# Attention and two feed-forward blocks in one program: batch 0's keys in three tiles of 128 and one shared tile, grouped loads of v, two leading products, one sum per pair, and a replanned order

## The chip, the core and the metric

The kernel runs on one core of a Trainium2 chip. The metric is the device time in microseconds (us) of one execution, compared as the median of several runs. The core's engines work side by side: TensorE (PE) multiplies matrices, with its weight loads listed apart (PEld), VectorE (DVE) and ScalarE (ACT) work on elements, GpSimd (POOL) and SyncE (SP) mostly issue transfers here. They wait for each other through semaphores, and each works through its own list of instructions in the order in which the program was written.

## The reference

Three blocks follow each other. `q`, `k`, `v` have 4 batches, 12 heads, 448 positions and 64 values a head; `cap` is 30.

```python
def _attn_ref(q, k, v, cap):
    scale = 1.0 / np.sqrt(q.shape[-1])
    scores = scale * np.matmul(q, k.transpose(0, 1, 3, 2))
    scores = cap * np.tanh(scores / cap)
    scores = scores - np.max(scores, axis=-1, keepdims=True)
    attn = np.exp(scores)
    attn = attn / (np.sum(attn, axis=-1, keepdims=True) + 1e-09)
    return np.matmul(attn, v).astype(np.float32)

def _moe_ref(x, w_in, w_out):        # 1792 x 768, 768 x 2048, 2048 x 768
    h = x @ w_in
    ...
    g = np.where(pos, h, np.where(neg, 0.0, (h + beta) ** 2 / (4.0 * beta)))
    return (g @ w_out).astype(np.float32)

def _moe2_ref(x, w1, w2, w3, w_out): # 1792 x 768, three of 768 x 768, 768 x 768
    h = np.maximum(np.maximum(x @ w1, x @ w2), x @ w3)
    return (h @ w_out).astype(np.float32)
```

## The kernel before

All work is transposed: positions (448 a batch) lie along a tile's free axis, features or keys along its 128 partitions.

*Attention* (`attention`, one call for each batch and pair of heads, 24 in all). The two heads of a pair lie on partitions 0 to 63 and 64 to 127. The 448 keys are cut into four tiles of 112. For each tile PE makes the scores of both heads (`score` in batch 0, as plain 32-bit products; `score_full` in the other batches, from values divided into a high and a low part), ACT takes tanh out of the PSUM buffer (`t`, 112 x 896) and then exp in place. PE then weighs v with the exps (`weigh`, accumulated in `ps_a`). For the denominator DVE adds the four exp tiles to one or two (`se`; the table `ADDED` says which: three adds to one tile in batches 0 and 3, two adds to two tiles in batches 1 and 2), and PE sums each over its partitions by a product with ones (`total4`, into `ps_r`; `total` for the last pair of batch 0). The sum with its epsilon (`rs`) is gathered by POOL to a small tile (`rc`), inverted on DVE, sent to device memory by SP and read back spread over 64 partitions a head (`spread2`). Last, `xf` is `ps_a` times `rs`, and it is divided into a high and a low part (`x`).

*Layers.* `ffn` runs the first block for batches 0 and 1; the later stages use a scheme with seven products of half matrices (`strassen`). A product of high precision is three products on PE of values in a shorter format (lines 899 to 901 and 1117): high by high, high by low, low by high. The weights come as 64-bit words and are turned to 32-bit numbers on DVE and ACT (`fetch_first`) and divided into two parts (`divided`: a cast on ACT or DVE, a subtraction on DVE). The first `PLAIN` = 6 units of `w_in` are not divided in batch 0: their six products each are plain 32-bit ones (line 894).

*Order.* Every piece of work is given to a planner (`Plan`) with a cost for each engine that could do it, a due time, what it depends on and which buffers it takes from pools of fixed size (`slots`). `run` steps through time, hands free engines the earliest due work that is ready, and `emit` writes all instructions in the order found. So a changed cost moves instructions on every engine up to the end. A dependency between engines is counted `LATENCY` later. PSUM pool `s` has two buffers for scores, `m` three for sums, weighings and layer products, `a` one. In batch 0, pairs 1, 2, 4 and 5 weigh into a buffer of `m`, which their `xf` frees.

*Start.* ACT loads `cap`, SP the keys and queries of the first pair, every engine loads the value of `cap` to a register (line 218) and branches on it; `cap` of 30 takes the branch without a maximum.

## Time and profile before

| | us |
|---|---|
| median of 3 runs | 955.91 (955.85 to 959.21) |
| the profiled execution | 959.17 |
| its span in the profile | 957.4 |
| PE busy | 937.2 (98%) |
| DVE busy | 778.0 (81%) |
| ACT busy | 594.5 (62%) |

The profiled execution is 1.8 us longer than its span, and 3.3 us longer than the median. "Busy" counts the time in which at least one instruction of the engine is under way. The page shows the span in 40 slices as well: PE's busy tenths read 7789999... and then 9 up to the last slice, so PE has idle time almost only in the first 70 us, which hold batch 0's attention. The granted clock (the share of TensorE's full clock) reads 9989 in the first four slices and 9 afterwards.

### The profile page before, as it was taken

How to read it: one execution, taken by the hardware profiler on the slowest of the kernel's cores; microseconds unless marked ns; L12 is line 12 of the kernel's file. 1: busy time of each engine (PE TensorE's matmuls, PEld its weight loads, DVE VectorE, ACT ScalarE, POOL GpSimd, SP SyncE). 2: the span in 40 equal slices, each digit the busy share in tenths (PEclk: the TensorE clock that was granted, in tenths of full speed). 3: DMA queues.
4: the chain of work that ended last, by engine and by line, in shares of the span. 5: the costliest groups of instructions: out<-in, count | busy, mean ns of one | idle time of the engine just before them, and what ended most of it. 6: DMA issues, size and time to landing. Idle time of an engine off the chain costs nothing.

```text
span 957.4 us, 14768 instructions
## 1 busy us (share of the span) xinstructions
PE 937.2 (98%) x5323; PEld 755.6 (79%) x5323; DVE 778.0 (81%) x1288; ACT 594.5 (62%) x932; POOL 14.7 (2%) x27
## 2 busy tenths in 40 slices
PE   7789999999999999999999999999999999999997
PEld 1134788777767676678999999999999999899997
DVE  2898898897989888888888848887889869758782
ACT  7968888775888877774434316566865715233441
POOL 0000000000000000000000000000000000000000
PEclk9989999999999999999999999999999999999999
DMA  7758768998888998853777887442233345446343
GB/s 201 220 154 267 236 191 245 274 287 270 291 280 279 302 292 259 232 173 118 253 265 271 288 295 255 123 140 80 90 101 109 111 121 184 144 147 205 108 148 120
DMA packets 95339, 194.48 MB, mean 203 GB/s; under 512 B 12094, under 2 KB 56858, under 8 KB 95258
## 3 DMA queue, kind: packets, MB, share of 16 engines
q1 hardware_dynamic: 94378, 193.36, 64.0%
q8 instruction: 44, 0.72, 0.3%
q0 software_dynamic: 736, 0.10, 0.1%
q14 instruction: 37, 0.30, 0.1%
q10 hardware_dynamic: 144, 0.00, 0.0%
HBM read 142.51 MB, written 50.81 MB: 202 GB/s over the span
## 4 chain that ended last, share of the span: by engine, by line
PE 90%; DMA 3%; DVE 3%; issue 2%; ACT 1%; SPq 0%; POOL 0%; DVEq 0%; ACTq 0%; POOLq 0%
PE ps_m L1117 32%; PE ps_s L1117 11%; PE ps_m L899 9%; PE ps_m L901 8%; PE ps_m L900 8%; PE ps_a L836 6%; PE ps_s L615 5%; PE ps_a L1117 5%; PE ps_m L894 3%; PE ps_r L709 1%; DMA qk<-in_qk 1%; DMA rc<-rs 1%; DVE op L315 1%; DVE se L315 1%; PE ps_s L626 1%
## 5 line engine op out<-in xcount | busy, mean ns | idle before, releaser
L1117 PE MATMUL ps_m<-op,w 128*128 128x448 f32 x1575 | 324.0, 365 | 0.6 <-DVE M L315 0.6
L1117 PEld LDWEIGHTS ps_m<-op,w 128*128 128x128 f32 x1575 | 295.7, 188 | 24.4 <-DVE M L315 1.0
L315 DVE TENSOR_TENSOR w<-wf,w 128x512 fp32r<-128x512 f32 (+2 forms) x155 | 117.6, 761 | 13.8 <-ACT w L310 11.4
L310 ACT ACTIVATE w<-wf 128x512 fp32r<-128x512 f32 (+2 forms) x120 | 81.1, 679 | 70.4 <-PE ps_m L1117 30.9
L633 ACT ACTIVATE t<-ps_s,qscale 112x896 f32<-112x896 f32 x96 | 93.4, 1004 | 33.0 <-PE ps_s L615 25.2
L1117 PE MATMUL ps_s<-op,w 128*128 128x448 f32 x522 | 110.7, 366 | 0.4 <-DVE op L315 0.2
L1117 PEld LDWEIGHTS ps_s<-op,w 128*128 128x128 f32 x522 | 98.0, 188 | 8.7 <-ACT op L310 0.5
L680 ACT ACTIVATE t<-t,cap_sb 112x896 f32<-112x896 f32 x96 | 95.9, 1038 | 0.3
L310 ACT ACTIVATE w<-ss 128x384 fp32r<-128x384 f32 (+1 forms) x93 | 53.1, 583 | 64.9 <-PE ps_m L1117 37.5
L836 PE MATMUL ps_a<-t,v 112*32 112x448 f32 (+1 forms) x752 | 79.4, 543 | 5.2 <-ACT t L680 2.7
L899 PE MATMUL ps_m<-g,w 128*128 128x448 f32 x192 | 72.6, 378 | 0.0
L315 DVE TENSOR_TENSOR w<-ss,w 128x384 fp32r<-128x384 f32 (+1 forms) x98 | 59.8, 627 | 14.3 <-ACT w L310 14.0
L901 PE MATMUL ps_m<-g,w 128*128 128x448 f32 x192 | 70.3, 366 | 0.0
L900 PE MATMUL ps_m<-g,w 128*128 128x448 f32 x192 | 70.3, 366 | 0.0
L836 PEld LDWEIGHTS ps_a<-t,v 112*32 112x32 f32 (+1 forms) x752 | 22.2, 110 | 51.3 <-issue 33.1
L899 PE MATMUL ps_m<-x,w 128*128 128x448 f32 x156 | 58.7, 376 | 0.0
L423 DVE SCALAR_TENSOR_TENSOR raw<-raw 128x768 int32<-128x768 int32 (+1 forms) x64 | 55.4, 867 | 3.0 <-ACT raw L412 2.5
L900 PE MATMUL ps_m<-x,w 128*128 128x448 f32 x156 | 57.1, 366 | 0.6 <-DVE x L315 0.6
L439 DVE SCALAR_TENSOR_TENSOR wf<-raw 128x768 int32<-128x768 int32 (+1 forms) x64 | 54.7, 856 | 3.1 <-ACT raw L431 1.6
L901 PE MATMUL ps_m<-x,w 128*128 128x448 f32 x156 | 57.0, 366 | 0.0
L1117 PE MATMUL ps_a<-op,w 128*128 128x448 f32 x234 | 51.3, 365 | 0.0
L1117 PEld LDWEIGHTS ps_a<-op,w 128*128 128x128 f32 x234 | 44.0, 188 | 3.5
(142 smaller groups left out, 1424.8 us busy)
## 6 DMA issues: line engine op xcount, KB each, us to landing
wf<-w SPq DMA_DIRECT2D x104, 192.0 KB
wf<-w SPq DMA_DIRECT2D x66, 256.0 KB
w<-wf SPq DMA_DIRECT2D x40, 384.0 KB
wf<-w SPq DMA_DIRECT2D x40, 384.0 KB
raw<-in_w SPq DMA_DIRECT2D x18, 768.0 KB
w<-p SPq DMA_DIRECT2D x36, 384.0 KB
raw<-in_w_in SPq DMA_DIRECT2D x16, 768.0 KB
raw<-in_w_out SPq DMA_DIRECT2D x24, 512.0 KB
```

The costliest lines, as they stand in the source:

```text
L310: nc.scalar.activation(out=out_, in_=in_, func=AF.Copy)
L315: nc.vector.tensor_tensor(out=out_, in0=a, in1=b, op=o)
L423: nc.vector.scalar_tensor_tensor(out=lo, in0=hi, scalar=-(2**31), in1=lo, op0=ALU.bitwise_and, op1=ALU.bitwise_or,)
L439: nc.vector.scalar_tensor_tensor(out=wf.tile[:, :n].bitcast(I32), in0=hi, scalar=3, in1=lo, op0=ALU.logical_shift_left, op1=ALU.bitwise_or,)
L615: nc.tensor.matmul(ps.tile[:C, j, :S], k.tile[o, 1, c * C : (c + 1) * C], q.tile[o, 0], start=n == 0, stop=n == 2,)
L633: nc.scalar.activation(out=t[c].tile, in_=ps.tile[:C, :, :S], func=AF.Tanh, scale=qscale[:C])
L680: lambda e, c=c: nc.scalar.activation(out=t[c].tile, in_=t[c].tile, func=AF.Exp, scale=cap_sb[:C]),
L836: nc.tensor.matmul(pa.tile[j * D + d : j * D + d + n, :S], vt.tile[:, j, c, d : d + n], t[c].tile[:, j], start=start, stop=stop,)
L899: nc.tensor.matmul(ps.tile[:, :S], wh, a.tile[:, 0], start=start, stop=False)
L900: nc.tensor.matmul(ps.tile[:, :S], wh, a.tile[:, 1], start=False, stop=False)
L901: nc.tensor.matmul(ps.tile[:, :S], wl, a.tile[:, 0], start=False, stop=stop)
L1117: nc.tensor.matmul(get(), w_, x_, start=start and z == 0, stop=stop and z == 2, skip_group_check=begun,)
```

## The change

Batch 0 alone (`HALVED`) takes its keys differently: the first 64 keys of both heads share one tile `th` (head 0 on partitions 0 to 63, head 1 on 64 to 127, 448 wide), and the other 384 lie in three tiles of 128. So a pair has three wide tiles and one of half the width where it had four of 112 partitions. `th` is scored and weighed by two products, one a head, in place of four. For the denominator DVE makes two adds (three wide tiles to one), and PE sums two tiles: `se` with ones, and `th` with `blocks`, which holds ones for one head's partitions and zeros for the other's.

v of batch 0 is loaded for three pairs at a time into a buffer of pool `w` (`load_thirds`), eight transfers each with runs of 64 values, in place of one transfer a pair with runs of 256 values.

Two products of ones by ones, which nothing reads, stand on PE ahead of all else. `PLAIN` is 3. `ADDED` is 3 in all batches: batches 1 and 2 make three adds and one sum a pair, where they made two and two. Pool `u` has 34 buffers (35), `h` 11 (9).

The planner counts an ACT pass as 0.1 us shorter and a DVE pass 0.08 us shorter for what follows on the same engine (`LAP`), a dependency 0.09 us later, also between passes of one engine other than PE, and a pause of 5 us after each gather and of 2 us after each read back.

```diff
--- before.py
+++ after.py
@@ -27,7 +27,8 @@
...
-    LATENCY = 0.08
+    LATENCY = 0.09
+    LAP = {"A": 0.1, "D": 0.08}
...
@@ -153,7 +154,7 @@
...
-                        free_at[e] = t + c
+                        free_at[e] = t + c - self.LAP.get(e, 0.0)
...
@@ -181,7 +182,7 @@
...
-                            d.t1 + (0.0 if d.e in x.cost and len(x.cost) == 1 else self.LATENCY)
+                            d.t1 + (0.0 if d.e == "T" and "T" in x.cost else self.LATENCY)
...
@@ -215,9 +216,21 @@
...
+    ones = const.tile([128, 64], F32, name="ones")
+    nc.vector.memset(ones, 1.0)
+    with (
+        tc.tile_pool(name="idle", bufs=1) as idle,
+        tc.tile_pool(name="ps_idle", bufs=1, space=bass.MemoryType.PSUM) as ps_idle,
+    ):
+        x, y = idle.tile([128, 448], F32, name="x"), ps_idle.tile([64, 448], F32, name="y")
+        nc.vector.memset(x, 1.0)
+        for _ in range(2):
+            nc.tensor.matmul(y, ones, x, start=True, stop=True)
     bits = nc.values_load(cap.bitcast(I32)[0:1, 0:1])
-    ones = const.tile([v.shape[2], 64], F32, name="ones")
-    nc.vector.memset(ones, 1.0)
+    blocks = const.tile([128, 2, 64], F32, name="blocks")
+    nc.gpsimd.memset(blocks, 0.0)
+    for j in range(2):
+        nc.gpsimd.memset(blocks[j * 64 : (j + 1) * 64, j], 1.0)
...
@@ -271,22 +284,23 @@
...
     FULL = (1, 2, 3)
+    HALVED = (0,)
     RC = 16
-    PLAIN = 6
+    PLAIN = 3
...
-    ADDED, FOURS, POOLED = (3, 2, 2, 3), (0, 1, 2, 3), ()
+    ADDED, FOURS, POOLED = (3, 3, 3, 3), (0, 1, 2, 3), ()
...
-    slots = {"u": 35, "h": 9, "v": 3, "w": 4, "wf": 5, "raw": 3, "rc": 2, "s": 2, "a": 1, "m": 3}
...
+    slots = {"u": 34, "h": 11, "v": 3, "w": 4, "wf": 5, "raw": 3, "rc": 2, "s": 2, "a": 1, "m": 3}
...
@@ -564,6 +578,46 @@
...
+    def load_thirds(b, a, begin):
+
+        vt = buf("w", "vt", [P, 3 * 7 * D])
+        src = v[b, 6 * a : 6 * a + 6]
+        ops = [[] for _ in range(NCH)]
+
+        def load(r, to, part):
+            q = op(
+                {"Q": 0.5}, lambda e: nc.sync.dma_start(out=to(vt.tile), in_=part),
+                begin + 0.1 * r, takes=[] if ops[0] else [vt], uses=[vt],
+            )
+            ops[r].append(q)
+
+        for r in range(NCH - 1):
+            first = D + P * r
+            for k in sorted({first, *(k for k in range(0, S, C) if first < k < first + P)}):
+                c, p = divmod(k, C)
+                n = min(first + P - k, C - p)
+                x = k - first
+                load(
+                    r,
+                    lambda t_, x=x, n=n, r=r: t_[x : x + n, r * 6 * D : (r + 1) * 6 * D].rearrange(
+                        "p (h d) -> p h d", d=D
+                    ),
+                    src[:, p : p + n, c].rearrange("h p d -> p h d"),
+                )
+        for j in range(2):
+            load(
+                NCH - 1,
+                lambda t_, j=j: t_[j * D : (j + 1) * D, 18 * D : 21 * D].rearrange(
+                    "p (i d) -> p i d", d=D
+                ),
+                src[j::2, :D, 0].rearrange("i p d -> p i d"),
+            )
+        return vt, ops
...
@@ -572,17 +626,42 @@
...
-        vt = buf("v", "v", [C, 2, NCH, D])
+        halved = b in HALVED
+        R = P if halved else C
+        if halved:
+            if i % 3 == 0:
+                thirds[i // 3] = load_thirds(b, i // 3, begin - (12 if i else -1))
+            vt, vls = thirds[i // 3]
+        else:
+            vt = buf("v", "v", [C, 2 * NCH * D])
...
-        t = [unit("t", rows=C) for _ in range(NCH)]
+        t = [unit("t", rows=R) for _ in range(NCH - 1 if halved else NCH)]
+        th = half("th") if halved else None
...
+        def v_part(j, c, d, n):
+            if halved:
+                o = (6 * c + 2 * (i % 3) + j) * D + d
+                return vt.tile[:, o : o + n]
+            o = (NCH * j + c) * D + d
+            return vt.tile[:, o : o + n]
+
+        def keys(k, j, c, first=0, n=R):
+            o = c * R + first
+            if halved:
+                o, n = (o + D, n) if c < NCH - 1 else (first, D)
+            return k[head_rows(j), 1, o : o + n]
...
@@ -602,36 +681,43 @@
...
-            def score(e, c=c, ps=ps):
-
-                for k in (0, D):
-                    n = min(D, C - k)
+            def score(e, c=c, ps=ps, tail=tail):
+                qk_ = qkt[0].tile
+                for k in (0,) if tail else (0, D):
+                    n = min(D, R - k)
                     for j in range(2):
-                        o = slice(j * D, (j + 1) * D)
+                        to = ps.tile[k : k + n, j, :S] if not tail else ps.tile[head_rows(j), 0, :S]
                         nc.tensor.matmul(
-                            ps.tile[k : k + n, j, :S],
-                            qkt[0].tile[o, 1, c * C + k : c * C + k + n], qkt[0].tile[o, 0],
-                            start=True, stop=True,
+                            to, keys(qk_, j, c, k, n), qk_[head_rows(j), 0], start=True, stop=True
                         )
...
-            def tanh(e, c=c, ps=ps):
+            def tanh(e, c=c, ps=ps, tail=tail):
+                if tail:
+                    nc.scalar.activation(
+                        out=th.tile, in_=ps.tile[:, 0, :S], func=AF.Tanh, scale=qscale
+                    )
...
@@ -639,8 +725,14 @@
...
-                s = op({"T": SCORE}, score, begin + c * SCORE, [ql], qkt, [ps], "rows")
-            tanhs.append(op({"A": 1.0}, tanh, begin + c * SCORE + 0.5, [s], [ps], [t[c]]))
+                s = op(
+                    {"T": SCORE / 2 if tail else SCORE}, score, begin + c * SCORE, [ql], qkt, [ps],
+                    "rows",
+                )
+            tanhs.append(op(
+                {"A": 0.6 if tail else 1.0}, tanh, begin + c * SCORE + 0.5, [s], [ps],
+                [th if tail else t[c]],
+            ))
...
@@ -668,19 +766,27 @@
...
+            x = th if halved and c == NCH - 1 else t[c]
...
             exps.append(op(
-                {"A": 1.03},
-                lambda e, c=c: nc.scalar.activation(
...
+                {"A": 0.62 if x is th else 1.03},
+                lambda e, x=x: nc.scalar.activation(
+                    out=x.tile, in_=x.tile, func=AF.Exp, scale=cap_sb[: P if x is th else R]
...
@@ -706,9 +812,11 @@
...
+                    w_, x_ = ones[:R, :32], src.tile[:, i // 2, o] if src is not th else None
+                    if src is th:
+                        w_, x_ = blocks[:, i // 2, :32], th.tile[:, o]
                     nc.tensor.matmul(
-                        pr.tile[i * 32 : (i + 1) * 32, : S // 2], ones[:, :32],
-                        src.tile[:, i // 2, o], start=start, stop=stop,
+                        pr.tile[i * 32 : (i + 1) * 32, : S // 2], w_, x_, start=start, stop=stop,
...
@@ -720,15 +828,20 @@
...
-        if ADDED[b] == 0:
+        if halved:
+            se = unit("se", rows=R)
+            sm = add(t[0], t[1], se, w, exps[:2])
+            sm = add(se, t[2], se, w + 0.1, [sm, exps[2]])
+            srcs = [(se, sm), (th, exps[3])]
...
             srcs = []
...
@@ -799,7 +912,7 @@
...
-            r = op({"S": 3.0 if first else 5.0}, lambda e: None, w + 0.06, [r], [rc, src])
+            r = op({"S": 5.0}, lambda e: None, w + 0.06, [r], [rc, src])
...
@@ -810,9 +923,8 @@
...
-            recips.append(
-                op({"Q": 0.7}, spread2, w + 0.3, [r], [rs], [rs] if pooled else [])
-            )
+            r = op({"Q": 0.7}, spread2, w + 0.3, [r], [rs], [rs] if pooled else [])
+            recips.append(op({"S": 2.0}, lambda e: None, w + 0.3, [r], [rs]))
...
@@ -830,11 +942,19 @@
...
+                if c == len(t):
+                    for j in range(2):
+                        nc.tensor.matmul(
+                            pa.tile[head_rows(j), :S], vt.tile[head_rows(j), (18 + i % 3) * D : (19 + i % 3) * D],
+                            th.tile[head_rows(j)],
+                            start=start, stop=stop,
+                        )
+                    return
...
@@ -844,13 +964,14 @@
...
-                {"T": STEP}, weigh(c), w + 0.1 * c, [exps[c], vl, avs[0]], [t[c], vt, pa],
-                kind=cols_kind,
+                {"T": STEP}, weigh(c), w + 0.1 * c, [exps[c], *vls[c], avs[0]],
+                [t[c] if c < len(t) else th, vt, pa],
+                kind=cols_kind if c < len(t) else "rows",
...
```

The built programs show where instructions went. First PE from its start, before and after (`y` is what the two new products write, `qk0_0` the first pair's keys and queries):

```order
L218 TENSOR_LOAD in_cap_ptr
L218 TENSOR_LOAD in_cap
L230 REGISTER_ALU
L230 COMPARE_AND_BRANCH
L626 MATMUL ps_s_265<-qk0_0_58 64x448 x2
L626 MATMUL ps_s_265<-qk0_0_58 48x448 x2
```

```order
L228 MATMUL y_72<-x_71,ones_63 64x448 x2
L229 TENSOR_LOAD in_cap_ptr
L229 TENSOR_LOAD in_cap
L243 REGISTER_ALU
L243 COMPARE_AND_BRANCH
L709 MATMUL ps_s_282<-qk0_0_58 64x448 x4
L709 MATMUL ps_s_291<-qk0_0_58 64x448 x4
```

The two products stand ahead of the loads of the value of `cap` and of the branch; the first score follows the branch in both.

Next PE at the first pair's weighing and sum, before and after (`ps_a` weighing, `ps_r` sums, `qk_272` and `qk_316` are pair 1's keys and queries):

```order
L836 MATMUL ps_a_302<-t_280,v_270 32x448 x4
L836 MATMUL ps_a_302<-t_282,v_270 32x448 x4
L626 MATMUL ps_s_320<-qk_272 64x448 x2
L626 MATMUL ps_s_320<-qk_272 48x448 x2
L836 MATMUL ps_a_302<-t_300,v_270 32x448 x4
L626 MATMUL ps_s_333<-qk_272 64x448 x2
L626 MATMUL ps_s_333<-qk_272 48x448 x2
L836 MATMUL ps_a_302<-t_325,v_270 32x448 x4
L709 MATMUL ps_r_350<-se_311,ones_70 32x224 x4
```

```order
L956 MATMUL ps_a_319<-t_296,vt_287 32x448 x4
L956 MATMUL ps_a_319<-t_300,vt_287 32x448 x4
L956 MATMUL ps_a_319<-t_314,vt_287 32x448 x4
L947 MATMUL ps_a_319<-th_335,vt_287 64x448 x2
L818 MATMUL ps_r_348<-se_326,ones_63 32x224 x4
L818 MATMUL ps_r_348<-th_335,blocks_85 32x224 x4
L709 MATMUL ps_s_359<-qk_316 64x448 x4
L709 MATMUL ps_s_370<-qk_316 64x448 x4
```

Before, pair 1's first two score tiles stand between pair 0's weigh steps; now they stand behind all of them and behind both sums.

Last DVE late in batch 0, before and after (`xf_615` and `xf_709` are pair 1's, `se_638` pair 4's sum before, `se_697` pair 5's after, `raw` and `wf` weights, `rs` of line 767 or 880 the epsilon):

```order
L315 TENSOR_TENSOR xf_615<-ps_a_375,rs_456 128x448
L767 TENSOR_SCALAR rs_617<-ps_r_601,eps_sb_119 128x224
L312 CAST x_620<-xf_615 128x448
L315 TENSOR_TENSOR x_620<-xf_615,x_620 128x448
L315 TENSOR_TENSOR se_638<-t_572,t_582 112x896
L315 TENSOR_TENSOR se_638<-se_638,t_606 112x896
L315 TENSOR_TENSOR se_638<-se_638,t_636 112x896
L315 TENSOR_TENSOR xf_665<-ps_a_462,rs_538 128x448
```

```order
L880 TENSOR_SCALAR rs_677<-ps_r_656,eps_sb_136 128x224
L922 RECIPROCAL rc_618<-rc_618 56x16
L447 TENSOR_SCALAR raw_544<-raw_544 128x768
L329 TENSOR_TENSOR se_697<-t_652,t_661 128x896
L329 TENSOR_TENSOR xf_709<-ps_a_395,rs_461 128x448
L453 SCALAR_TENSOR_TENSOR wf_712<-raw_544 128x768
L329 TENSOR_TENSOR se_697<-se_697,t_695 128x896
```

Before, pair 1's `xf` stands ahead of pair 4's adds; now it stands behind the first add of pair 5.

## Rows read from the trace of the kernel before

**Rows 1.** The page, busy us, share of the span and instructions of each engine.
```profile
PE 937.2 (98%) x5323; PEld 755.6 (79%) x5323; DVE 778.0 (81%) x1288; ACT 594.5 (62%) x932; POOL 14.7 (2%) x27
```

**Rows 2.** Stretches: length, busy (instructions) by engine, granted clock, DMA share, GB/s.
```profile
50.00:60.00 10.00, 7.46 (x54) 1.88 (x52) 8.83 (x15) 7.47 (x8) 0.60 (x1) 0.94 0.52 150
...
60.00:70.00 10.00, 10.00 (x38) 5.06 (x35) 9.51 (x15) 6.72 (x9) 0.00 (x0) 0.71 0.49 135
...
100.00:450.00 350.00, 348.23 (x2277) 259.84 (x2274) 304.67 (x469) 275.51 (x383) 10.75 (x17) 1.00 0.81 251
...
120.00:140.00 20.00, 20.00 (x106) 17.67 (x103) 18.66 (x29) 18.96 (x28) 0.00 (x0) 1.00 0.53 167
...
450.00:500.00 50.00, 50.00 (x248) 46.34 (x247) 43.75 (x73) 19.09 (x31) 0.00 (x0) 1.00 0.73 250
```

**Rows 3.** Timeline of the start: start, length, engine, line, operation, [idle, releaser].
```profile
4.31 0.37 SPq L583 DMA_DIRECT2D v<-in_v  x1
...
4.34 4.70 PE L626 MATMUL ps_s<-qk 64*64 64x448 f32 x24 [4.34 <-DMA qk<-in_qk]
...
7.01 1.01 ACT L633 ACTIVATE t<-ps_s,qscale 112x896 f32<-112x896 f32 x1 [2.49 <-PE ps_s L626]
...
16.36 0.56 PE L709 MATMUL ps_r<-se,ones 112*32 112x224 f32 x8
```

**Rows 4.** Line 218: duration in ns, least, median and most, first and last start.
```profile
L218 PEldq TENSOR_LOAD <-in_cap_ptr x1: 921/921/921, 0.8 to 0.8; - x1
...
L218 PEldq TENSOR_LOAD <-in_cap x1: 656/656/656, 1.8 to 1.8; - x1
```

**Rows 5.** Timeline of batch 0's later pairs.
```profile
29.52 0.97 PE L626 MATMUL ps_s<-qk 64*64 64x448 f32 x8
...
31.31 1.72 PE L626 MATMUL ps_s<-qk 64*64 64x448 f32 x16
...
35.93 0.24 DVE L809 RECIPROCAL rc<-rc 56x16 f32<-56x16 f32 x1 [0.79 <-DMA rc<-rs]
...
46.01 0.62 DVE L315 TENSOR_TENSOR xf<-ps_a,rs 128x448 f32<-128x448 f32 x1 [1.24 <-DMA rs<-rc]
...
46.69 2.46 PE L836 MATMUL ps_a<-t,v 112*32 112x448 f32 x24 [2.49 <-DVE xf L315]
...
52.86 1.97 ACT L680 ACTIVATE t<-t,cap_sb 112x896 f32<-112x896 f32 x2
...
53.04 2.81 PE L836 MATMUL ps_a<-t,v 112*64 112x448 f32 x12
...
59.36 1.76 PE L695 MATMUL ps_r<-se,ones 112*64 112x448 f32 x4 [1.54 <-DVE se L315]
```

**Rows 6.** Timeline where the layers of batch 0 begin.
```profile
61.83 1.56 DVE L820 RECIPROCAL rs<-rs 128x112 f32<-128x112 f32 x2 [0.36 <-ACT rs L765]
...
67.82 0.46 PE L615 MATMUL ps_s<-qk_hi 64*112 64x448 f32 x2
...
69.22 22.07 PE L894 MATMUL ps_m<-xf,wf 128*128 128x448 f32 x58
...
91.22 0.96 PE L709 MATMUL ps_r<-se,ones 112*32 112x224 f32 x16
...
92.00 3.19 PE L836 MATMUL ps_a<-t,v 112*32 112x448 f32 x32
```

**Rows 7.** Groups of 60 to 450 us: busy us, mean ns, idle before.
```profile
L315 DVE TENSOR_TENSOR se<-t 112x896 f32<-112x896 f32 x30 | 32.2, 1081 | 1.8 <-ACT t L680 1.8
...
L894 PE MATMUL ps_m<-xf,wf 128*128 128x448 f32 x72 | 28.9, 559 | 0.0
...
L315 DVE TENSOR_TENSOR w<-wf,w 128x768 fp32r<-128x768 f32 x28 | 26.6, 952 | 0.6 <-ACT w L310 0.5
...
L935 ACT ACTIVATE u<-ps_m 128x448 f32<-128x448 f32 x27 | 14.4, 535 | 5.2 <-PE ps_m L901 3.9 <-PE ps_m L894 1.4
...
L312 DVE CAST w<-wf 128x512 fp32r<-128x512 f32 x11 | 4.6, 422 | 0.0
```

More of the change, by code (lines that the diff above doesn't have):

```diff
@@ L604, in attention @@
             parts3, got = ((hi_, hi_), (hi_, lo_), (lo_, hi_)), [hi, lo]
-        vl = op({"Q": 1.0}, load_v, begin + 1, takes=[vt])
+        if not halved:
+            vl = op({"Q": 1.0}, load_v, begin + 1, takes=[vt])
+            vls = [[vl]] * NCH
         tanhs = []
@@ L651, in attention @@
             )
-            for c in range(2, NCH):
+            for c in range(2, len(t)):
                 m0 = op(
@@ L657, in attention, with larger @@
                 )
+            for j in range(2 if halved else 0):
+                def larger(e, j=j):
+                    o = mx.tile[head_rows(j), j]
+                    tt(e, o, o, th.tile[head_rows(j)], ALU.max)
+                m0 = op(c_tt(KS), larger, w + 0.1, [m0, tanhs[-1]], [mx, th])
             def reduce(e):
@@ L846, in attention @@
             {"T": STEP}, weigh(0), w,
-            [vl] + (exps[:1] if first else exps if pooled else exps + sums),
+            vls[0] + (exps[:1] if first else exps if pooled else exps + sums),
             [t[0], vt], [pa], cols_kind,
```

54 lines of the change are left out of this document (33 added, 21 removed).

## The prediction

> **What bounds the kernel now.** I read the page's engine totals first: TensorE (PE) is busy for 937.2 of 957.4 us and VectorE (DVE) for 778.0 [rows 1]. So a gain has to come from PE's idle 20 us, from work taken off PE, or from its clock. The stretches show where each of these lies [rows 2]. From 450 to 500 us PE starts 248 products, one every 0.2016 us; from 100 to 450 it is busy for 348.23 of 350 us, with DVE at 304.67. Nearly all of the idle time lies in the first 60 us, the attention of batch 0. The granted clock is below full there as well: 0.94 in 50 to 60 us and 0.71 in 60 to 70, so (0.06 + 0.29) x 10 = 3.5 us of full-clock work is lost.
>
> The profiled execution took 959.17 us, the slowest run 959.21 and the median 955.91. The 3.3 us between them is about what that clock stretch costs. I take it that the two faster runs did not have it; no row shows this. My sum starts from the profiled execution and assumes no such stretch afterwards, so its end is compared with the median directly.
>
> Batch 0 is six pairs of heads. From the timeline [rows 5] two alternating PE steps (a score tile, then a weigh tile) take 31.31 - 29.52 = 1.79 us, 0.90 each; two equal ones take 0.86 each. ScalarE (ACT) does two exps in 1.97 us, some 0.95 a pass allowing for changes of kind. Before, a pair costs PE 8 x 0.88 + 0.5 = 7.5 us and ACT 8 x 0.95 = 7.6. They are level, and what is lost beside that is waits: PE waited 2.49 us at 46.69 us for the xf of pair 1 (released at 46.01, ten us after that pair's reciprocal at 35.93), and 1.54 us at 59.36 us for DVE's sum.
>
> The point of comparison at the end is the first layer product of batch 0. A plain product is two of the 58 records at 69.22 us, so (22.07 - 0.56) / 57 x 2 = 0.755 us [rows 6]; the 0.56 is one product's own time [rows 7]. Four of them were done before 67.82 us, so with everything else put ahead the plain products start at 69.22 - 4 x 0.755 = 66.2 us.
>
> **The change part by part.** *Start.* PE's 24 first records take 4.70 us [rows 3], where later ones take 0.97 for eight [rows 5]: with the wait for the second head's keys inside, PE starts at the lower of its two levels. The two unread products stand ahead of PE's value loads. Each is a plain product's size in columns, so 3.0 us for both at half clock; they begin after a memset of 448 columns (bounds 0.1 to 0.6 us after 0.8), at some 1.4 us, and end at 4.4, as the first keys arrive (4.34). If the clock then rises by about 5 us, the first tanh moves from 7.01 to 6.1. The value loads took 0.92 + 0.66 us on PE [rows 4]: if PE's queue holds them until the products end, the first tanh comes at 7.4 instead. I take 6.1, the end at which the keys' arrival decides as it does in the row of 4.34; both ends stay in the range.
>
> *First pair.* ACT has six wide passes and two half passes per pair: 6 x 0.95 + 2 x 0.55 = 6.8 us (0.535 us for a 448-column pass, rows 7). It ends at 12.9 us. In the new order pair 1's first score stands behind all of pair 0's weigh tiles and both its sums, so ACT then waits for 0.86 + 2 x 0.45 of PE: scores of pair 1 begin at 14.7 us.
>
> *Pairs 1 to 5.* The narrow key tile does not help PE. The 64-wide weigh steps of the last pair, two products in place of four, took 2.81 us for three [rows 5], 0.94 each: a step costs its columns, not its number of products. So a pair is still eight steps, and one more sum of about 0.45 (0.56 for one alone, rows 3): 8.0 us against ACT's 6.8. PE now sets the pace, and the 0.8 us that ACT saves a pair is worth nothing. Four pairs, less pair 4's weighing (3.4), plus pair 5's scores (3.5), bring PE to about 47 us.
>
> *Hand-over.* Pair 4's weighing needs the buffer that pair 1's xf frees. On DVE that xf now stands behind the first add of pair 5, which needs pair 5's second exp. ACT restarts at 15.6 us; four pairs of 6.8, one eps, one x and one qk_hi (1.95 together) and pair 5's first four passes end at 48.6; add 1.08 and xf 0.62: 50.3 us. PE waits some 3 us. Then: weigh 3.4, two score tiles of batch 1 (67.82 to 69.22 for two, so 1.4), two sums 1.7, two more tiles 1.4: 58.2 us. Pair 5's weighing waits for pair 2's xf, which DVE has behind eps, a scaling and a reciprocal, 2.6 us after the sums: 59.4. Four steps of 0.9: plain products start at 63.0 us. Against 66.2 that is **-3.2 us**.
>
> *Plain units 6 to 3.* 18 products of 0.755 become 18 of 3 x 0.2016 = 0.605: **-2.7 us** of PE. The three units' division (DVE 0.952 each for the low half, rows 7, and a cast) is done before those products come up, 20 us later.
>
> *One sum per pair in batches 1 and 2.* Two sums took 92.00 - 91.22 = 0.78 us on PE [rows 6]. Twelve of 0.39 go: **-4.7 us**. In their place come 12 adds of 1.081 us on DVE [rows 7].
>
> *Replanned order.* The planner now takes 0.1 us (ACT) and 0.08 us (DVE) off each pass. It moves casts: counting the built order, DVE gets 42 more casts of weights (about 0.42 each, 18 us), 13 us of adds and 3 of low halves, and loses 6.5 us in batch 0. DVE goes from 778 to about 805 us, ACT down by some 34. PE is the bound from 100 us on and DVE had 45 us free between 100 and 450, so most of it is hidden; bounds 0 and 15 us (the rival below). I take **+1 us**, nearest to the row: 1.8 us of PE idle in 350 us at 87% DVE.
>
> *Keys and v.* v for three pairs is eight transfers ahead of pair 1's keys. One took 0.37 us to issue [rows 3], so eight take 3 to 4.4, and pair 1's keys are issued by 8.7 us in place of 4.8; they are needed at 14.7. This costs nothing unless landing takes over 6 us. The runs of v shrink from 1 KB to 256 bytes. The Trainium skill ("DMA: Bandwidth & Descriptors", Specifications) has full line rate only from 512 bytes on. At the 251 GB/s of [rows 2] the 688 KB take 2.7 us, at half rate 5.5, and pair 0's last weigh tile could come 1 us late: the sum would be 950.5. No run here shows such runs of bytes.
>
> Sum: 959.2 - 3.2 - 2.7 - 4.7 + 1 = **949.6**; I predict 949.5.
>
> **The rivals.** *Round trips and the clock again, 955.* xf of pairs 1 to 4 depends on the reciprocals' way through memory, ten us in [rows 5]. If it takes a few us longer under the new transfers, PE's two waits (3 and 1.2 us) grow by 2 us, and an idle PE may be given the lower clock again, as at 60 us: +3.5. 949.5 + 5.5 = 955. For it: the waits are in the same place as before. Against: PE has fewer gaps before. The Trainium skill ("TensorE: Matmul & The Clock Gate", Part 1) says that the chip's watching is not in step with the kernel, so the same program may or may not meet the fall; the two kinds of times of the kernel before agree with that.
>
> *Better overlap, 944.* If the sums are hidden between steps and xf of pair 1 and 2 come in time (no 3 and 1.2 us waits, and some of ACT's saving shows), the plain products start near 57.5 us. Against: the order on DVE puts xf where I said.
>
> *DVE becomes the bound, 964 (slower).* Between 100 and 450 us DVE's 304.67 us grow by about 30 (adds, casts, divisions) to 335. The densest stretch, 120 to 140 us, has DVE at 18.66 of 20, 0.93. If that is all that in-order issue allows, the stage takes 335 / 0.93 = 360 us in place of 350 - 4.7 = 345: it decides as soon as DVE's work passes 0.93 x 345 = 321 us, and at 335 it costs 15 us where the sum has 1: 964. For it: ACT's relief is DVE's load, and the plan counts DVE as faster than before. Against: the deduction is right by a row (two reciprocals in 1.56 us at 0.82 each, rows 6), much of batch 1's added work lies in stretches under 0.9, and the stage with DVE's heaviest load kept PE busy.
>
> *The unread products do nothing.* If they hold PE's value loads or the clock falls again before the keys come, the first tanh is at 7.0 to 7.4: +1, inside the range.
>
> **How the numbers follow.** Forecast 949.5 (own range 945 to 953): 0.52. Round trips and clock, 955: 0.28. Better overlap, 944: 0.12. DVE the bound, 964: 0.08. What can be told from no change is 0.5%, 4.8 us: under 951.1 is faster, over 960.7 slower. Faster: the better overlap and most of the forecast (its range up to 951.1), 0.12 + 0.46 = 0.58. Slower: 0.08. Same: 0.34. The range 942 to 958 leaves out the slower rival and the edge of the better one.
>
> **What would show it.** Right: first tanh near 6.1 us; a gap in ACT of 2 to 3 us near 13 to 15; PE busy for 8 us a pair; PE's wait for pair 1's xf near 50 us; first plain product near 63; 18 plain products; PE's sum of layer work unchanged. Wrong: a first tanh after 7; PE idle over 4 us on DVE between 100 and 450 (then DVE is the bound); a granted clock below 1 after 45 us; or a transfer of keys that ends PE's wait at 15 us.

## The result and the profile after

The changed kernel took 947.84 us, the median of four runs (940.86, 942.50, 953.18, 954.12), beside 957.56, the median of four runs of the kernel before. The ratio is 0.9886, interval 0.9842 to 0.9931. The forecast was 949.5. Two of the four times lie near 942 and two near 954, with nothing between; the profiled execution is one of the long ones (953.18, span 951.3). So the median stands close to the forecast, but no single execution does, and most of what follows is about that.

The page's engine totals of the changed kernel, beside [rows 1]:

```profile
PE 938.8 (99%) x5249; PEld 758.2 (80%) x5249; DVE 787.8 (83%) x1339; ACT 562.0 (59%) x894; POOL 14.8 (2%) x30
```

ACT lost 32 us, DVE gained 10, and PE is busy for a little longer than before in a span that is 6 us shorter. That last number already says that the same products must have become dearer somewhere. The stretches (length, busy and instructions of PE, PEld, DVE, ACT, POOL, then granted clock, DMA share, GB/s), beside [rows 2]:

```profile
15.03:51.18 36.15, 33.87 (x321) 10.21 (x317) 24.02 (x36) 35.15 (x45) 3.15 (x5) 1.00 0.94 244
50.00:60.00 10.00, 9.41 (x57) 3.89 (x54) 10.00 (x17) 9.66 (x13) 0.18 (x1) 1.00 0.79 241
60.00:70.00 10.00, 10.00 (x28) 4.97 (x27) 10.00 (x15) 8.67 (x14) 0.00 (x0) 1.00 0.70 178
100.00:450.00 350.00, 348.60 (x2213) 262.50 (x2212) 320.45 (x502) 259.32 (x367) 10.29 (x17) 1.00 0.83 257
120.00:140.00 20.00, 20.00 (x127) 15.87 (x126) 19.52 (x32) 18.23 (x32) 0.61 (x1) 1.00 0.73 225
450.00:500.00 50.00, 50.00 (x243) 45.42 (x242) 44.34 (x77) 18.79 (x31) 0.00 (x0) 1.00 0.70 237
600.00:900.00 300.00, 300.00 (x1453) 272.49 (x1453) 243.52 (x463) 144.91 (x284) 0.00 (x0) 1.00 0.40 122
```

Three things are to be seen. The clock is 1.00 where before had 0.94 and 0.71. In the first row, the stretch of the pairs, ACT is busy for 35.15 of 36.15 us and PE for 33.87: both are nearly full, and ACT has the less idle time. And from 450 to 500 us PE starts 243 products where before it started 248, at full clock and with no idle time.

The timeline of the start, beside [rows 3] (start, length, engine, line, operation, what ended the idle time before):

```profile
1.47 3.25 PE L228 MATMUL y<-x,ones 128*64 128x448 f32 x4 [1.47 <-DVE x L226]
...
4.78 2.27 PE L709 MATMUL ps_s<-qk 64*64 64x448 f32 x16
...
6.37 1.91 ACT L719 ACTIVATE t<-ps_s,qscale 128x896 f32<-128x896 f32 x2 [1.76 <-PE ps_s L709]
...
13.24 0.97 PE L947 MATMUL ps_a<-th,vt 64*64 64x448 f32 x4 [0.27 <-ACT th L786]
...
15.03 1.73 PE L709 MATMUL ps_s<-qk 64*64 64x448 f32 x16
15.17 0.45 ACT L878 ACTIVATE rs<-ps_r,eps_sb 128x224 f32<-128x224 f32 x1 [1.98 <-PE ps_r L818]
...
16.08 1.91 ACT L719 ACTIVATE t<-ps_s,qscale 128x896 f32<-128x896 f32 x2 [0.47 <-PE ps_s L709]
```

The hand-over to the layers, beside [rows 5, 6]:

```profile
45.33 0.59 PE L818 MATMUL ps_r<-se,ones 128*32 128x224 f32 x8 [1.08 <-DVE se L329]
...
47.88 0.16 PEld L956 LDWEIGHTS ps_a<-t,vt 128*32 128x32 f32 x8 [0.71 <-DVE rs L880]
47.89 2.46 PE L956 MATMUL ps_a<-t,vt 128*32 128x448 f32 x24
...
50.43 0.61 DVE L329 TENSOR_TENSOR xf<-ps_a,rs 128x448 f32<-128x448 f32 x1
...
56.37 2.48 PE L956 MATMUL ps_a<-t,vt 128*64 128x448 f32 x12 [0.29 <-DVE rs L880]
...
59.68 2.52 PE L1015 MATMUL ps_m<-xf,wf 128*128 128x448 f32 x6
```

Pair 1's xf comes at 50.43, but pair 4's weighing is already under way at 47.89; its last wait was for rs, the pass that reads its own pair's sums out of PSUM. So, going by that wait, it takes in the new order the bank that those sums leave, not the one that pair 1's xf frees. The first plain product stands at 59.68.

Last, PE where the last two batches begin:

```profile
415.62 5.64 PE L1238 MATMUL ps_m<-op,w 128*128 128x448 f32 x27
421.94 3.21 PE L956 MATMUL ps_a<-t,v 112*32 112x448 f32 x32 [0.68 <-DVE xf L329]
425.09 111.86 PE L1238 MATMUL ps_m<-op,w 128*128 128x448 f32 x540
```

The first op product was at 434.08 us before and is at 415.62 now, but the last one is at 945.78 beside 951.86: of 18.5 us only 6.1 reach the end. 3.1 us of this is one pair's weighing (the row of 421.94), which the new order puts behind the first op products. Most of the rest is the third row: (111.86 - 0.37) / 539 = 206.8 ns from one product to the next. I took the mean over all steps of 180 to 230 ns between neighbouring op products: 206.6 ns after, 202.7 before. Over 2330 products that is 9 us. The theory to test: there are two such distances, one of which holds from one break of PE's stream to the next, and the long one fell on this execution by chance. The rival: the new order or its transfers cause it.

### The profile page after: what moved, and what is told of

It is laid out like the page before. It is cut to its first block, busy times and chain, and to the rows that moved or that the text cites. A ratio compares the mean times of both kernels' runs of the same rounds, so it can differ in the third digit from the quotient of the medians.

```text
span 951.3 us, 14610 instructions
## 1 busy us (share of the span) xinstructions
PE 938.8 (99%) x5249; PEld 758.2 (80%) x5249; DVE 787.8 (83%) x1339; ACT 562.0 (59%) x894; POOL 14.8 (2%) x30
## 4 chain that ended last, share of the span: by engine, by line
PE 66%; issue 25%; DMA 3%; DVE 2%; ACT 2%; POOL 0%; SPq 0%; POOLq 0%; DVEq 0%
PE ps_m L1238 34%; PE ps_s L1238 11%; PE ps_a L1238 5%; PE ps_m L1020 3%; PE ps_m L1022 3%; PE ps_m L1021 3%; PE ps_a L956 3%; DMA rc<-rs 2%; PE ps_m L1015 1%; PE ps_s L698 1%; ACT t L719 1%; ACT t L786 1%; DMA w<-wf 1%; POOL rc L901 0%; DVE se L329 0%
## 5 line engine op out<-in xcount | busy, mean ns | idle before, releaser
L1238 PE MATMUL ps_m<-op,w 128*128 128x448 f32 x1575 | 330.2, 368 | 0.0
L329 DVE TENSOR_TENSOR w<-wf,w 128x512 fp32r<-128x512 f32 (+2 forms) x158 | 119.8, 760 | 2.9 <-ACT w L324 1.8
L719 ACT ACTIVATE t<-ps_s,qscale 112x896 f32<-112x896 f32 (+1 forms) x90 | 87.0, 1008 | 31.8 <-PE ps_s L698 29.4
L324 ACT ACTIVATE w<-wf 128x512 fp32r<-128x512 f32 (+2 forms) x97 | 67.5, 696 | 58.2 <-PE ps_m L1238 28.4
L786 ACT ACTIVATE t<-t,cap_sb 112x896 f32<-112x896 f32 (+1 forms) x90 | 90.1, 1044 | 0.0
L324 ACT ACTIVATE w<-ss 128x384 fp32r<-128x384 f32 (+1 forms) x77 | 43.7, 575 | 59.8 <-PE ps_m L1238 33.7
L1020 PE MATMUL ps_m<-x,w 128*128 128x448 f32 x174 | 65.8, 378 | 0.0
L1021 PE MATMUL ps_m<-x,w 128*128 128x448 f32 x174 | 63.7, 366 | 0.0
L1022 PE MATMUL ps_m<-x,w 128*128 128x448 f32 x174 | 63.7, 366 | 0.0
L326 DVE CAST w<-wf 128x512 fp32r<-128x512 f32 (+2 forms) x61 | 27.9, 458 | 39.3 <-DMA wf<-w 11.2
L956 PE MATMUL ps_a<-t,v 112*32 112x448 f32 x576 | 57.7, 541 | 0.8 <-DVE xf L329 0.7
```

The source lines that it names most:

```text
L324: nc.scalar.activation(out=out_, in_=in_, func=AF.Copy)
L326: nc.vector.tensor_copy(out_, in_)
L329: nc.vector.tensor_tensor(out=out_, in0=a, in1=b, op=o)
L719: nc.scalar.activation(out=t[c].tile, in_=ps.tile[:R, :, :S], func=AF.Tanh, scale=qscale[:R])
L786: lambda e, x=x: nc.scalar.activation(out=x.tile, in_=x.tile, func=AF.Exp, scale=cap_sb[: P if x is th else R]),
L956: nc.tensor.matmul(pa.tile[j * D + d : j * D + d + n, :S], v_part(j, c, d, n), t[c].tile[:, j], start=start, stop=stop,)
```

## The experiments: the last two batches

**again.** The changed kernel with nothing altered.

> The changed kernel once more, nothing altered. Theory A (the distance from one layer product to the next in the last two batches is one of two values, 202.7 or 206.7 ns, fixed by chance at the last break of TensorE's stream and then kept): the runs' times spread between 940.5 and 954.5 us, near both ends and not near their middle alone, and a profiled run of 941 to 943 us shows a mean of about 202.7 ns over the 2330 products, one of 952 to 955 shows 206.6. Rival B (the new order or its transfers slow TensorE down there): every profile shows 206.6 ns and what differs between runs of 941 and 953 us lies elsewhere, in the first 100 us.

Six runs: 941.19, 942.30, 942.35, 943.05, 943.63 and 954.46. The profiled one took 943.63. Its stretch, to be set beside the last row of the stretches above:

```profile
600.00:900.00 300.00, 300.00 (x1482) 278.39 (x1481) 248.84 (x475) 145.54 (x286) 0.00 (x0) 1.00 0.43 129
```

1482 products where the long execution started 1453, so 202.4 ns in place of 206.5 by these counts, from the same instructions. The last two batches begin at 416.02 us, 0.4 later than in the long execution, and end 9.7 us earlier. The rival is out: the order is the same. The prediction's comparison can now be made like with like: 943.63 against 959.17, both with the short distance, is -15.5 us.

**breaks.** A narrow product ahead of every group of the last two batches, whose result the real product overwrites:

```
+ if start and banks is six_banks:
+     nc.tensor.matmul(get()[:, :64], wh, h[:, :64], start=True, stop=True)
```

> In the last two batches one more product of 64 columns stands ahead of each group's first product in stages A11 and A12; the real product overwrites what it leaves. Theory A: each one breaks the even stream for some 0.1 to 0.2 us and the distance is drawn anew, so both 202.7 and 206.7 ns occur between 450 and 950 us in one run, in stretches that begin at such breaks, and the mean is 203.5 to 206; the runs' times lie closer together than 12 us (945 to 953). Rival B: 206.6 ns from 450 to the end as in the profiled run of the changed kernel, with times 2 to 6 us above it.

948.83 to 954.71, median 950.73, and the profiled execution has both distances (the second row counts narrow products as well; the trace has 69, all of them from 582 us on):

```profile
440.00:530.00 90.00, 90.00 (x438) 81.77 (x437) 76.73 (x131) 30.12 (x49) 0.00 (x0) 1.00 0.75 248
600.00:900.00 300.00, 300.00 (x1507) 279.01 (x1506) 243.66 (x463) 145.72 (x285) 0.00 (x0) 1.00 0.40 122
```

The 90 us of the first row hold 438 products, as in the long execution (206.7 ns between neighbours), where the short one has 446. The long distance ends at 582.66 us, at the first narrow product, and does not return at any later one. So it is not drawn anew each time, as the expectation had it: the narrow product ends it. Two of the six times, 954.04 and 954.71, lie above the range given (945 to 953).

**few_breaks.** The same in at most ten places (the trace shows eight), the first of them in the layer that begins at 415 us:

```
+ narrow = g < 2 and stage == 0 and i == 0 and k == 0
  ...
+ if narrow:
+     nc.tensor.matmul(get()[:, :64], wh, h[:, :64], start=True, stop=True)
```

> The changed kernel with one more product of 64 columns, whose result is overwritten, ahead of the first product of the first two groups of each of the five layers of the last two batches: at most ten in all, at 0.1 us each. Theory A (a narrow product between even ones sets the shorter distance, as it did in the run with one at every group, where 206.7 ns ended at the first one and never came back in 69): all runs lie between 941.5 and 945.5 us, none over 950, and the profile shows 202.7 ns from 435 us on. Rival (each break draws anew, 206.7 ns about three times in ten): some runs lie between 946 and 955, and 206.7 ns occurs after 435 us in stretches that begin and end at the narrow products.

Six runs from 942.39 to 943.97, median 943.05; ratio to before 0.9842, interval 0.9806 to 0.9877. PE at the place in question (L1240 is the narrow product):

```profile
424.72 5.84 PE L1244 MATMUL ps_m<-op,w 128*128 128x448 f32 x27
430.39 0.19 PE L1240 MATMUL ps_m<-op,w 128*128 128x64 f32 x1
430.42 9.76 PE L1244 MATMUL ps_m<-op,w 128*128 128x448 f32 x47
```

The long distance had begun in this execution too: of the 27 products behind the weighing of 421 us all but the first two steps are 206 or 207 ns. They end at 430.39 with the narrow product, and from there to the end it is 202.7. Theory A of this run holds, in one trace directly and in six times out of six. The spread of 13 us is gone, and the median lies 0.7 us above the 942.35 of the seven short executions of the kernel without narrow products, with spreads that overlap. Why a narrow product does it no run tells.

One thing more can be read from the traces. The two distances are no property of the change or of the last two batches. The timeline of the kernel before, PE alone, shows an unbroken row of its layer products (lines 899 to 901 in turn) and the sum that ends it:

```profile
147.96 0.37 PE L899 MATMUL ps_m<-x,w 128*128 128x448 f32 x1
...
167.79 0.37 PE L899 MATMUL ps_m<-g,w 128*128 128x448 f32 x1
...
168.50 0.96 PE L709 MATMUL ps_r<-se,ones 112*32 112x224 f32 x16
```

From the first of these rows to the second it is 96 steps in 19.83 us, some 206.6 ns each; behind the sum and the weighing that follow it, the next such rows have 202.7. Between 60 and 415 us the fourteen profiles hold 339 unbroken rows of eleven products or more, and 67 of them have the long distance, at least one in every profile. There scores, sums and weighings break the stream every few microseconds, so it costs little. In the last two batches of the long execution no such break comes any more, and it costs 9 us. Directly behind a narrow product the long distance was not found once, neither behind the 69 of breaks nor behind the 32 in the four profiles with few of them.

**before_breaks.** The same lines in the kernel before.

> The kernel before with the same ten or fewer narrow products of 64 columns (first product of the first two groups of each layer of the last two batches), nothing of the change. Theory A (the longer distance strikes the kernel before as well, in about one run of six, and a narrow product ends it): all runs between 954 and 961 us, none at 962 to 966 as 6 of 37 runs of the kernel before had. Rival (the runs of 962 to 966 have another cause, the falls of the clock before 70 us or later): they still occur, or the median falls by more than 2 us.

Ten runs from 956.01 to 961.41, median 957.78, ratio 1.0019 (1.0005 to 1.0033). None at 962 to 966, but the 18 runs of the kernel before beside it (953.78 to 959.18) had none either, so this says nothing on which cause those six had. It does say that the narrow products alone gain nothing in the kernel before.

## The experiments: the parts of the change

Here times are compared among executions without the long distance, or by where the last two batches begin (416.02 us in the profile of the repeated changed kernel, which is the reference for this section; its first plain product is at 59.50).

**keys112.** Batch 0 with four key tiles of 112 and its own v: `HALVED = (0,)` becomes `()`.

> Batch 0 goes back to four key tiles of 112 and v of one pair at a time; all else of the change stays (the two unread products, the new plan, three plain units, one sum per pair). Theory A (ScalarE sets the pace of batch 0's pairs, and the narrow tile takes 0.8 us off its pair): the pairs go from 7.0 to about 7.7 us and the first plain product comes 3 to 5 us later, at 63 to 65 us. Rival (TensorE sets the pace, since a narrow step costs as much as a wide one, as predicted): one sum per pair falls away on TensorE, and the first plain product is at 58 to 60.5 us, no later than now (59.7).

948.19 to 950.31, median 948.53, about 6 us above 942.4, the median of the changed kernel's seven short executions. The last two batches begin at 421.69, 5.7 us later. By its letter the rival came true, since the first plain product is at 58.03; but then PE stands still for the xf of later pairs (timeline, then stretches):

```profile
62.27 5.53 PE L1015 MATMUL ps_m<-xf,wf 128*128 128x448 f32 x14 [1.72 <-DVE xf L329]
...
69.81 0.62 DVE L329 TENSOR_TENSOR xf<-ps_a,rs 128x448 f32<-128x448 f32 x1
...
70.49 2.04 PE L1015 MATMUL ps_m<-xf,wf 128*128 128x448 f32 x4 [2.68 <-DVE xf L329]
```
```profile
15.00:52.00 37.00, 33.54 (x334) 9.34 (x328) 32.85 (x46) 37.00 (x43) 3.15 (x5) 1.00 0.87 265
...
70.00:80.00 10.00, 9.51 (x25) 5.33 (x26) 9.25 (x13) 7.14 (x12) 0.00 (x0) 0.83 0.89 297
```

ACT is busy for all of the 37 us, PE for 33.54: here ACT sets the pace. From pair 1's first tanh to pair 5's it takes 7.7 us a pair (14.41 to 45.27), where the changed kernel takes 7.1 (16.08 to 44.51), as theory A had it. The last xf of batch 0, pair 4's, comes at 69.81 in place of 65.95; that pair's sums already began 3.2 us later (49.01 in place of 45.86). PE loses 4.4 us in the two waits and (1 - 0.83) x 10 = 1.7 us by the clock, less the 1.5 by which its plain products begin earlier: 4.6 of the 5.7 us. So the narrow tile's shorter ACT passes do count, and the mark I had chosen, the first plain product, was the wrong one. The edit also takes away a sum a pair and brings another order on every engine; how much of the 5.7 us is the order's no run tells.

**plain6.** `PLAIN = 3` becomes 6.

> Six plain units again in place of three, all else of the change stays. Theory A (18 products cost 0.74 us each plain and 0.605 in three parts): TensorE needs 2.4 to 3.2 us more between the first plain product and the last two batches, 358.5 to 360 us, and the first plain product stays at 59.5 to 60. Rival (VectorE and ScalarE, relieved of three divisions, give some of it back, or the plain products start earlier): under 1.5 us in all.

Four times of 943.55 to 953.52, median 946.84; the last fits the long distance. From the first plain product (59.83) to the last two batches PE takes 362.13 us, but here the pair's weighing of 3.14 us comes before that mark; without it 359.0, against 356.5: 2.5 us. Theory A, by that correction; the prediction said 2.7.

**two_sums.** `ADDED = (3, 3, 3, 3)` becomes `(3, 2, 2, 3)`.

> Two sums per pair again in batches 1 and 2, all else of the change stays. Theory A (TensorE is the bound there): it needs 4.0 to 5.0 us more between the first plain product and the last two batches, 360 to 361.5 us. Rival (the adds cost VectorE as much as TensorE gains): under 2 us more, since waits for VectorE go away, or even less than now.

946.38 to 950.07, median 947.04. PE's time on sums in that stretch is 13.05 us in place of 8.59, so 4.46 (prediction: 4.7), and the last two batches begin 4.3 us later. Between the marks of the expectation it is 361.6 us, 5.1 more, since the first plain product comes 0.8 earlier: just past the upper end given. Theory A in the main.

**before_one_sum.** The same number the other way round, in the kernel before: `(3, 2, 2, 3)` becomes `(3, 3, 3, 3)`.

> The kernel before with one sum per pair in batches 1 and 2, nothing else of the change. Theory A (only the new plan makes room on VectorE for the 12 further adds): TensorE's time for the sums falls by 4.5 us but its waits for VectorE between 100 and 434 us grow, and the median falls by under 2 us or rises. Rival (the adds are hidden under the old plan as well): the last two batches begin 4 to 5 us earlier, at 429 to 430 us, and the median is 3.5 us or more below that of the kernel before.

959.94 to 964.40, median 960.20 beside 956.41: slower by 0.5%, ratio 1.0053 (1.0032 to 1.0074). The waits of PE between 130 and 150 us (engine, tile, releaser: total, times, longest), and the stretch behind the wait:

```profile
PE ps_r L709 <- DVE se L315: 3.3, 1, 3.3
```
```profile
140.00:150.00 10.00, 9.50 (x59) 4.14 (x60) 6.53 (x11) 5.03 (x9) 0.61 (x1) 0.66 0.66 186
```

The add is late on DVE, PE stops for 3.3 us, and the granted clock of the stretch is 0.66, which is another 3.4 us of full-clock work. What PE saves on sums goes there. Theory A, on the side of "rises".

**old_plan.** The planner's old numbers and rule, all else changed:

```
- LATENCY = 0.09
- LAP = {"A": 0.1, "D": 0.08}
+ LATENCY = 0.08
+ LAP = {}
- d.t1 + (0.0 if d.e == "T" and "T" in x.cost else self.LATENCY)
+ d.t1 + (0.0 if d.e in x.cost and len(x.cost) == 1 else self.LATENCY)
```

> The planner's three old numbers (latency 0.08, nothing taken off a pass, the old rule of which waits are free), all else of the change stays. Theory A (it is the new order that brings pair 1's and pair 2's xf in time): TensorE waits again for DVE's xf, 2 us or more near 45 to 60 us, and the first plain product comes at 62 us or later. Rival (the order is worth 1 us or less, as predicted): first plain product at 59 to 61 us, and TensorE's work between it and the last two batches takes 356 +- 1 us as now.

955.11 to 966.19, median 957.99, ratio to before 1.0020 (0.9986 to 1.0053): with this order nothing is left of the gain. Both expectations failed. The first plain product is at 59.04, so the changed numbers aren't what brings xf in time; but up to the last two batches PE needs 365.2 us in place of 356.5. Its waits from 60 to 450 us, and one stretch:

```profile
PE ps_r L818 <- DVE se L329: 3.8, 3, 2.8
PE ps_s L698 <- ACT t L719: 1.9, 3, 0.9
PE ps_m L1238 <- DVE M L329: 1.8, 1, 1.8
PE ps_m L1020 <- DVE rs L880: 0.6, 1, 0.6
```
```profile
430.00:440.00 10.00, 8.22 (x33) 7.17 (x33) 9.21 (x18) 4.32 (x9) 0.00 (x0) 0.83 0.47 172
```

8.1 us of waits, where the changed kernel's long execution has 1.3, and a clock below 1 after the two longest, at 108 and 435 us. The largest is again a sum that waits for the add. From 100 to 450 us DVE is busy for 308.62 us here, less than the 320.45 of the changed kernel. The old numbers give a third order and not that of the kernel before (the pauses after gathers and read backs stay), so the 8.2 us by which the last two batches begin later are what the new order is worth against this one; which of the three numbers does it was not tried.

**no_unread** and **no_unread_breaks.** The two unread products left out, and the same with the few narrow products:

```
- for _ in range(2):
-     nc.tensor.matmul(y, ones, x, start=True, stop=True)
+ nc.vector.memset(y, 0.0)
```

> The two unread products are left out (a write of zeros to their bank stands in their place on VectorE), all else of the change stays. Theory A (they are worth what they take off the first tanh, because TensorE then reaches its upper clock earlier): the first tanh comes at 7.0 to 7.6 us in place of 6.4 to 6.6, the clock rises about a microsecond later, and the first plain product comes 0.4 to 1.0 us later, at 60.0 to 60.7. Rival (what is gained at the first tanh is lost again in the wait before pair 1's scores): first plain product at 59.4 to 59.9.

> The changed kernel with the few narrow products but without the two unread products at the start. Theory A (what they gain at the first tanh, 0.5 us, is lost before pair 1's scores and the first plain product stands at 59.6 to 59.8 either way): median within 0.7 us of 943.05. Rival (the earlier clock is worth what the first tanh gains, 0.5 to 1 us, or more where the clock rises late): median 943.6 to 945.

The first gave 942.89 to 944.50 in three runs and 952.27 to 954.91 in seven, so its median of 952.50 tells of the distance and not of the products (whether these change how often the long one comes, 7 of 10 beside 3 of 10, is open). The second gave 943.24 to 944.49, median 943.88 of four, beside 943.05 with them: within 0.9 us, just outside theory A's bound, from two sets of runs whose spreads overlap. The trace of the first:

```profile
4.45 6.56 PE L708 MATMUL ps_s<-qk 64*64 64x448 f32 x28 [4.45 <-DMA qk<-in_qk]
...
7.05 1.01 ACT L718 ACTIVATE t<-ps_s,qscale 128x896 f32<-128x896 f32 x1 [2.45 <-PE ps_s L708]
...
16.31 1.74 PE L708 MATMUL ps_s<-qk 64*64 64x448 f32 x16
```

Pair 1's scores are 1.28 us later than with the unread products (15.03), but the first plain products are at 59.73 and 59.26, beside 59.50 and 59.68. What is gained at the start is lost again before 60 us. A gain of up to 0.8 us isn't excluded; none is shown. Of the two kernels with few narrow products, no execution of ten (six and four) was a long one; of the same two without them, ten of twenty had times that fit it.

**plain0.** To see whether the direction goes on: few_breaks with `PLAIN = 0`.

> The changed kernel with the few narrow products and no plain unit: all of batch 0's products in three parts. Theory A (each of the 18 remaining plain products costs TensorE 0.13 us more, and the divisions of three more units by VectorE and ScalarE fit beside batch 0's attention): median 1.5 to 3 us below that with three plain units (943.05), 940 to 941.5. Rival (VectorE has no room for three more divisions before 60 us, so the first layer product or the sums and xf come later): first layer product later than 61 us and a median of 943 us or above.

947.10 to 950.90, median 948.11, 5 us slower. The rival's verdict, but at another place: the first layer product comes at 59.16, no later than now. PE's waits from 125 to 240 us, and one stretch:

```profile
PE ps_r L818 <- DVE se L329: 2.8, 1, 2.8
PE ps_s L698 <- DVE qk_lo L329: 1.6, 1, 1.6
```
```profile
130.00:140.00 10.00, 8.14 (x60) 4.02 (x60) 9.88 (x17) 6.85 (x12) 0.61 (x1) 0.83 0.67 210
```

In this order DVE's add and a division of qk (`qk_lo`) come after the point where PE wants them, and behind each stop the clock falls (the second at 234 us). That the further divisions push them there is likely, but the planner moved other work too.

## Why the prediction was right, and where it was not

*The time.* 949.5 is right for the median of four and close to none of them. Two errors of opposite sign met: attention 3.4 us better than said, the order some 3 us better, and in half of those runs 9 us or more lost to a distance that the prediction did not have. Of the ten runs of the unaltered kernel seven lie at 940.9 to 943.6; the range's lower end (942) cuts through them.

*Start.* First tanh 6.37 (6.1 predicted; 6.2 to 7.1 in nine profiles with unread products). The value loads did not hold anything up, but the keys' arrival did not decide either. PE's first score starts at 4.78, 0.06 us behind the end of the unread products (1.47 + 3.25 = 4.72), with no wait for a transfer; without them the same transfer ends PE's wait at 4.45 (no_unread). So the products cost some 0.3 us there and gain more in this profile, where the first tanh is at 6.37 beside 7.05 without them. The step was carried on to pair 1's scores as a gain, and nothing of it is left at the first plain product.

*First pair.* Scores of pair 1 at 15.03 (14.7), the gap in ACT 1.98 + 0.47 us (2 to 3): right.

*Pairs 1 to 5.* "PE now sets the pace" at 8.0 us a pair is wrong in part. The stretch from 15.03 to 51.18 us holds PE's scores of five pairs and the weighing and sums of four: 33.87 us of work, where I had 4 x 8.0 + 3.5 = 35.5. A pair's two sums take 0.89 (14.14 to 15.03 us), so a step is (33.87 - 3.6) / 36 = 0.84 us and a pair 7.6. I took 0.9 us for every step, a step's price where scores and weighing alternate; the new order groups more equal ones, and the 24 weigh records at 47.89 take 2.46 us for three steps, 0.8 each. These 1.6 us are half of what the plain products came early. ACT, with 1.0 us of idle time beside PE's 2.3, is the tighter of the two, and the 0.8 us a pair that I had called worth nothing show in ACT's period (keys112).

*Hand-over.* xf of pair 1 was predicted for 50.3 us and came at 50.43, but the 3 us wait for it did not: pair 4's weighing no longer depends on it. I had carried a dependence on a buffer over from the old trace into a new allocation. Pair 5's weighing started at 56.37, not 59.4, and the plain products at 59.5 to 59.7, not 63.0. Against the same work before (66.2) that is -6.6 in place of -3.2. Of the 6.6, (0.06 + 0.29) x 10 = 3.5 us is the clock stretch of [rows 2], which the changed kernel does not have; some 3 us are left for the attention itself. The sum assumed that the stretch is gone but had no term for it: of its -3.2, nothing would have been left for the attention.

*Plain units, sums.* -2.5 and -4.5 measured, -2.7 and -4.7 predicted. But the sums' gain was entered as if it stood alone. In the kernel before's order it isn't there: by the medians it costs 3.8 us (before_one_sum).

*Replanned order, +1.* This term had the wrong sign and size. It was read as a price, moved work that is "mostly hidden". The -15.5 us of the like comparison less 6.6, 2.5 and 4.5 leave -1.9 for it. With the old numbers in place of it the last two batches begin 8.2 us later. The rival in which DVE becomes the bound describes just what happens then, and its mechanism (adds late, PE's sums waiting) is real in three of the kernels run here. I had DVE's work at 335 us between 100 and 450; it is 320.45, in part because I added up single passes, and these overlap at their ends where one follows the other (over the whole run their lengths grew by 21.5 us, the busy time by 9.8; I had 27). That is at the 321 where I had it decide, with 19.52 of 20 from 120 to 140 us, and still PE waits for 1.3 us only, while in old_plan, with DVE at 308.62, PE waits for 8.1, 6.2 of them for DVE. So a busy share of 0.93 is no limit by itself; what counts here is the place of the awaited pass in DVE's queue.

*Keys and v.* Nothing was late: pair 0's last weighing (13.24) waits for ACT and not for a transfer. The Trainium skill ("DMA: Bandwidth & Descriptors", Specifications) has full line rate only from 512 bytes on, and the prediction's estimate from it was up to 1 us for v's runs of 256 bytes; the trace shows no such wait.

*What would show it.* 18 plain products (36 records at 59.68 to 72.94) and no clock below 1 after 45 us: as said. "PE's sum of layer work unchanged" was the sign that failed, through the long distance.

*Left open.* I took the 3.3 us between the kernel before's runs for one stretch of lower clock. Its 55 runs beside the experiments lie between 953.5 and 960.7 us without a step, but for six at 962 to 966; none of the six has a profile. But the mean granted clock of each is on record: 0.995 to 0.997 for the six and 0.995 to 0.999 for the others, so a lower clock is not what sets the six apart. Among the other 49 it does a part of what I assumed: the eight at 0.995 have a mean of 957.4 us, the eleven at 0.998 or 0.999 one of 955.2. That the six are runs with the long distance would fit by size and is not shown.

## What to carry to other kernels

An edit that takes work off the bound engine by giving it to another can be worth nothing until the order on that other engine lets it come in time: try it with the replanning and without. Read what a step costs from the order it will have, not from the one it had, and ask which buffer it takes there. When the times of one kernel fall into two groups, compare the distance between its most frequent instructions in a trace of each group before explaining a mean. And when a mark (here the first plain product) is taken for a stage, look whether the order lets it come before the stage is done.

## What the hardware showed

The same stream of 448-column products, each with its weight load of 188 ns, at a granted clock of 1.00 and with no idle time, runs at 202.7 or at 206.7 ns a product. Which of the two it is was settled at a break of the stream and held to the next: the long one for 2518 products in one execution, for some 755 in breaks and for 27 in few_breaks, where a 64-column product ended it. Behind breaks by other work 67 of 339 rows were long, behind a 64-column product none. In all, 3 of 10 runs of the changed kernel had times that fit it.

Some stops of PE went with a stretch at the lower level (1.2 GHz) that began between 0.6 us before their end and 1.4 us after it: 2.7 us in keys112, 2.8 and 1.8 in old_plan, 3.3 in before_one_sum, and 2.8 and 1.6 in plain0. A stop of 1.7 us in keys112 (62.27) did not, nor did the kernel before's stop of 2.49 us (46.69 in [rows 5]). The Trainium skill ("TensorE: Matmul & The Clock Gate", Part 1) says that the chip's watching is not in step with the kernel, and that fits a stop of 1.6 us with a fall beside stops of 1.7 and 2.49 without.
